# Pooled attention and a GELU layer: scores of 64 pools of both token kinds in one matmul, the other 8 pools in column tiles, k turned by a transposing DMA

## The chip, the core and the metric

The kernel runs on one core of a Trainium2 chip. A core has TensorE (PE, matmuls; a separate record PEld for its weight loads), ScalarE (ACT), VectorE (DVE), GpSimd (POOL) and SyncE (SP). SP, ACT and POOL can issue DMA transfers. The metric is the device time of one execution in microseconds. The kernel before takes 307.78 us (median of three runs, 307.62 to 308.16).

## The reference

Eight batches, eight heads, 576 tokens, head size 64. k and v are averaged over groups of 8 tokens, which gives 72 pools. Then attention of every token over the 72 pools, and a layer with GELU over all 4608 tokens:

```
k_p = k.reshape(B, H, 72, 8, 64).mean(axis=3)       # v_p likewise
scores = 1/sqrt(64) * q @ k_p.T                      # [576, 72] per batch and head
attn = exp(scores - max) / sum
x = (attn @ v_p), heads side by side: [4608, 512]
h = x @ w_in                                         # [4608, 2048]
out = gelu_tanh(h) @ w_out                           # [4608, 512]
```

## The kernel before

**Layout.** `xT` holds the attention's result with the 512 features on partitions (four blocks `ko`, one for each pair of heads) and all tokens along the row. The layer runs over nine groups `g` of 512 tokens. In each group a first product (`p1_mm`, line 332: 16 blocks `fo` of 128 hidden features, four matmuls each, 512 tokens wide), the GELU of each block (`gelu`, line 338, on ScalarE, PSUM to `gT`), and a second product (`p2_mm`, line 343: four blocks of 128 tokens, 16 matmuls each), whose result `store` (line 349) copies to `osb` on VectorE and sends out in four DMAs from SP.

**Attention beside it.** While group `g` is worked on, batch `nb = g + 1` goes through its attention, for g = 0 to 6. Batch 0 has its own code ahead of the loop. In the first product's part, VectorE sums k and v over 8 tokens (`k_steps`, `v_steps`; plan at lines 467 to 473) in three halving additions; TensorE transposes the summed k (`trans_k`, line 196: five transposes), and VectorE copies them into `kTs`. There are two copies of `kT` for a batch, one for each token kind `c` (even and odd tokens): q is transposed in pieces of 128 columns, which are two tokens of 64 features, so even tokens sit on partitions 0 to 63 and odd ones on 64 to 127, and the `kT` of the other half is zero. One transfer, `trans_q_dma` (line 221), transposes q on SP for batches 2 and up.

In the second product's part the matmuls of attention are laid between those of `p2_mm` at written positions `m` (0 to 63; lines 506 to 517; `seq` and `todo`). For each (c, pr), pr being a pair of heads: `qk` (line 234) gives the scores of two heads into PSUM banks 2 and 3, two matmuls 288 tokens wide; `expo` takes exp on ScalarE; `av` (line 254) multiplies by v, whose weights carry 8.0 in 64 further columns, so that one matmul gives both the sum over pools and the denominator, into banks 4 and 5 or 6 and 7 by turns; `norm` (line 265) makes the reciprocal on ScalarE by two logarithms and an exponential; `mult` (line 273) writes `xT` on VectorE in two halves. Heads 4 to 7 have their v sums on partitions 64 to 127, and use 128 rows of pools with zeros between (`pool_rows`).

**Order.** The order on each engine is that of the program text. Tiles carry semaphores, and an engine waits at the instruction that needs one. ScalarE loads a table of functions at each change between GELU and exp (`act_set`). Banks for the products: `h_bank` (line 319) and `o_bank`.

**Loads.** `load_next` (line 449) issues the loads of batch g + 2: q, then its transpose, then a one-element copy on POOL (`gate`) that waits for the transpose, then k, the last 8 pools of v, and the rest of v. All of these loads are issued by POOL. `load_v(1)` (line 422) is issued by SP after a one-column memset during the start-up. `v_moves` (line 148) moves the last 8 pools of v between partitions, in two small DMAs on SP.

The last block of the last group is computed in two column ranges, of 384 and 128 columns; each is stored by four DMAs, two on SP and two on ACT.

The softmax here doesn't subtract the row's maximum and nothing guards it: scores larger than these inputs give would overflow.

## Time and profile before

| what | value |
|---|---|
| median of three runs | 307.78 us |
| profiled execution: its own time | 307.9 us |
| its span in the profile | 306.1 us |
| PE busy | 296.8 us (97%), 1528 matmuls |
| ACT busy | 219.0 us (72%) |
| DVE busy | 150.5 us (49%) |
| POOL busy | 35.0 us (11%) |
| granted TensorE clock | 1.0 of full speed |
| DMA | 41.12 MB, 30806 packets |
| software queue (POOL), SP's queue, ACT's queue | 24.38, 15.14 and 1.31 MB |

The span runs from the first to the last instruction that the profile records; the execution's own time is 1.8 us longer. A matmul's busy time is modelled, and matmuls overlap, so what a stage costs is read from the starts of matmuls in the timeline. A group line gives the line of the code, the engine, the operation, the output and input tiles with their sizes, the count, busy time and mean ns. A timeline line gives start, length, engine, line and operation, and in brackets how long the engine stood idle ahead of it and what released it. The DMA view gives the packets of each queue within a window: q0 is the software queue that POOL feeds, q1 belongs to SP, q10 to ACT.

### The profile page before, as it was taken

How to read it: one execution, taken by the hardware profiler on the slowest of the kernel's cores; microseconds unless marked ns; L12 is line 12 of the kernel's file. 1: busy time of each engine (PE TensorE's matmuls, PEld its weight loads, DVE VectorE, ACT ScalarE, POOL GpSimd, SP SyncE). 2: the span in 40 equal slices, each digit the busy share in tenths (PEclk: the TensorE clock that was granted, in tenths of full speed). 3: DMA queues.
4: the chain of work that ended last, by engine and by line, in shares of the span. 5: the costliest groups of instructions: out<-in, count | busy, mean ns of one | idle time of the engine just before them, and what ended most of it. 6: DMA issues, size and time to landing. Idle time of an engine off the chain costs nothing.

```text
span 306.1 us, 4354 instructions
## 1 busy us (share of the span) xinstructions
PE 296.8 (97%) x1528; PEld 157.6 (51%) x1557; DVE 150.5 (49%) x336; ACT 219.0 (72%) x402; POOL 35.0 (11%) x67
## 2 busy tenths in 40 slices
PE   8999899999999999999999999999999999999994
PEld 3555455555555555555555555555555555445543
DVE  5885757572577057805682559245932630120012
ACT  1687489867987798779977898789868986206500
POOL 7102002305003200320014000400000000000000
PEclk9999999999999999999999999999999999999999
DMA  7999987977955962696159827672101210121022
GB/s 221 266 254 264 227 171 139 310 168 184 257 138 113 278 154 53 118 279 154 35 112 250 181 61 103 203 153 71 35 1 36 59 44 0 36 70 35 2 68 69
DMA packets 30806, 41.12 MB, mean 134 GB/s; under 512 B 18176, under 2 KB 18432, under 8 KB 29888
## 3 DMA queue, kind: packets, MB, share of 16 engines
q0 software_dynamic: 7568, 24.38, 33.7%
q1 hardware_dynamic: 22528, 15.14, 21.1%
q10 hardware_dynamic: 688, 1.31, 1.3%
q8 instruction: 12, 0.20, 0.3%
q14 instruction: 10, 0.08, 0.1%
HBM read 36.70 MB, written 9.44 MB: 151 GB/s over the span
## 4 chain that ended last, share of the span: by engine, by line
PE 87%; DMA 11%; issue 1%; ACT 0%; DVE 0%; POOLq 0%
PE PS L344 40%; PE PS L335 37%; DMA qb<-in_q_dram 11%; PE PS L238 5%; PE PS L260 4%; PE PS L173 1%; PE PS L203 0%; ACT e L246 0%; ACT ld L268 0%; ACT ld L267 0%; DVE osb L353 0%; POOLq L550 0%
## 5 line engine op out<-in xcount | busy, mean ns | idle before, releaser
L344 PE MATMUL PS<-w_out_b,gT 128*128 128x512 bf16 (+2 forms) x577 | 133.9, 373 | 0.7
L335 PE MATMUL PS<-xT,w_in_b 128*128 128x512 bf16 x563 | 126.6, 379 | 0.7
L341 ACT ACTIVATE gT<-PS 128x512 bf16<-128x512 f32 x144 | 81.2, 603 | 48.1 <-PE PS L335 48.0
L335 PEld LDWEIGHTS <-w_in_b 128*128 128x128 bf16 x576 | 64.7, 113 | 57.2
L344 PEld LDWEIGHTS <-gT 128*128 128x128 bf16 x592 | 57.0, 97 | 55.7 <-issue 0.4
L353 DVE COPY osb<-PS 128x512 f32<-128x512 f32 (+2 forms) x37 | 25.1, 677 | 98.2 <-PE PS L344 78.6
L278 DVE TENSOR_TENSOR xT<-PS,rc 64x288 bf16<-64x288 f32 x112 | 50.9, 455 | 31.7 <-ACT rc L270 27.5
L246 ACT ACTIVATE e<-PS 72x576 bf16<-72x576 f32 (+1 forms) x64 | 41.0, 647 | 8.8 <-PE PS L238 7.9
L238 PE MATMUL PS<-qT,kT 128*72 128x288 bf16 (+1 forms) x128 | 25.8, 286 | 0.9 <-ACT qT L213 0.6
L270 ACT ACTIVATE rc<-ld 128x288 f32<-128x288 f32 x56 | 24.8, 444 | 1.8
L313 ACT ACT_TABLE_LOAD x17 | 21.8, 1283 | 4.3 <-issue 4.1
L267 ACT ACTIVATE ld<-PS 64x288 f32<-64x288 f32 x56 | 22.8, 408 | 1.3
L268 ACT ACTIVATE ld<-PS 64x288 f32<-64x288 f32 x56 | 22.5, 402 | 1.4
L260 PE MATMUL PS<-e,vp 72*128 72x288 bf16 (+1 forms) x112 | 23.1, 286 | 0.0
L138 DVE TENSOR_TENSOR kt<-kt 128x1280 f32<-128x1280 f32 (+5 forms) x18 | 18.9, 1048 | 7.6 <-DMA kt<-in_v_dram 4.6
L238 PEld LDWEIGHTS <-kT 128*72 128x72 bf16 (+1 forms) x128 | 13.2, 105 | 15.1 <-DVE qT L215 1.2
L453 POOL COPY gate<-qT 1x2 bf16<-1x2 bf16 x6 | 1.0, 174 | 138.5 <-DMA qT<-qb 138.5
L138 DVE TENSOR_TENSOR vt<-vt 128x1024 f32<-128x1024 f32 (+1 forms) x16 | 15.3, 956 | 1.7 <-DMA vt<-in_v_dram 1.4
L183 DVE COPY kT<-PS 64x288 bf16<-64x288 bf16 (+2 forms) x48 | 13.0, 318 | 6.2 <-PE PS L173 6.0
L260 PEld LDWEIGHTS <-vp 72*128 72x128 bf16 (+1 forms) x112 | 11.0, 98 | 3.8
L365 PE MATMUL PS<-idle 128*128 128x512 bf16 x32 | 10.4, 468 | 1.6 <-DVE idle L126 1.2
L76 POOL DMA_DIRECT2D kt<-in_v_dram x14 | 8.0, 586 | 0.1
(48 smaller groups left out, 88.8 us busy)
## 6 DMA issues: line engine op xcount, KB each, us to landing
out_dram<-osb SPq DMA_DIRECT2D x140, 64.0 KB
kt<-in_k_dram POOLq DMA_DIRECT2D x7, 1024.0 KB, 6.0
vt<-in_v_dram POOLq DMA_DIRECT2D x12, 512.0 KB, 8.7
qb<-in_q_dram POOLq DMA_DIRECT2D x7, 576.0 KB, 11.8
w_in_b<-in_moe_w_in_dram POOLq DMA_DIRECT2D x2, 1024.0 KB, 16.8
w_out_b<-in_moe_w_out_dram POOLq DMA_DIRECT2D x4, 512.0 KB, 19.3
vt<-in_v_dram SPq DMA_DIRECT2D x3, 512.0 KB
kt<-in_k_dram POOLq DMA_DIRECT2D x7, 128.0 KB, 6.0
```

Of the source, the lines that this page charges most:

```text
L138: nc.vector.tensor_tensor(out=o, in0=a, in1=b, op=ALU.add)
L238: nc.tensor.matmul(out=PS[:n, bank + e, :CH].rearrange("j (t p) -> j t p", p=32), lhsT=kTs[b % 2][c][:, h, :n], rhs=qTs[b][:, h // 4, :, h ...
L246: nc.scalar.activation(out=e[:n], in_=PS[:n, bank:bank + 2, :CH], func=ACT.Exp, scale=1.0 / 64.0)
L260: nc.tensor.matmul(out=PS[:, bank + x, :CH], lhsT=window(vps[b % 2][:n], 2 * pr + x), rhs=e[:n, x, :], start=True, stop=True)
L267: nc.scalar.activation(out=ld[0:64], in_=PS[64:128, bank, :CH], func=ACT.Ln)
L268: nc.scalar.activation(out=ld[64:128], in_=PS[0:64, bank + 1, :CH], func=ACT.Ln)
L270: nc.scalar.activation(out=rc, in_=ld, func=ACT.Exp, scale=-1.0)
L278: nc.vector.tensor_tensor(out=xT[rows, pr, col:col + CH], in0=PS[rows, bank + x, :CH], in1=rc[rows], op=ALU.mult)
L335: nc.tensor.matmul(out=PS[:, h_bank(g, fo), c0:c1], lhsT=w_in_b[fo // 8][:, ko, q * 512 + j:(q + 1) * 512:4], rhs=xT[:, ko, r0 + c0:r0 + c ...
L341: nc.scalar.activation(out=gTs[g][:, fo, :], in_=PS[:, h_bank(g, fo), :], func=ACT.Gelu_apprx_tanh)
L344: nc.tensor.matmul(out=PS[:, bank, c0:c1], lhsT=gTs[g][:, fo, r * 128:(r + 1) * 128], rhs=w_out_b[:, fo, c0:c1], start=(fo == 0), stop=(fo ...
L353: nc.vector.tensor_copy(out=osb[:, c0:c1], in_=PS[:, bank, c0:c1])
```

## The change

Batches 0 and 1 keep the old path, with 72 rows of pools for all heads (`pool_rows` is gone, v sums of heads 4 to 7 are written to partitions 0 to 63, and `kTs`, `vps`, `vz` and `ones` shrink to match). For batches 2 to 7 (`KX = 2`):

- k is loaded with its first 64 pools on partitions, four heads on each half, in rows of 2 KB (`load_k_dma`); VectorE writes its sums twice into `kz` (64 partitions), so that each head has a block for even and one for odd tokens with zeros in the other half; one transposing DMA on SP turns all of it into `kx` (`trans_k_dma`). The five TensorE transposes and the copies into `kTs` go.
- `main_scores`: for each head one matmul with 128 columns of weights gives the scores of the first 64 pools for even tokens (rows 0 to 63) and odd tokens (rows 64 to 127). `main_expo` writes its exponentials into rows 0 to 63 of `eT`, for one token kind at a time.
- `rem_scores`: the last 8 pools, eight matmuls (one for each head) of 16 columns of weights, written at partitions 0, 32, 64 and 96 of banks 6 and 7. `rem_expo`: one exponential over all of it, then eight DMAs on SP that move the rows to partitions 64 to 71 of `eT`.
- `av_main` is `av` on `eT`, with pairs of heads in the outer order and token kinds in the inner. Positions `m` are new; the last `av_main` comes after the second product.
- `load_next` for batches 3 and up is issued in the first product's part, after the k sums; its gate waits for `kx`, and q comes last; q's transpose is issued on SP at m = 30.
- In the start-up, `load_v(1)` comes after four more memsets, and v of batch 1 is summed in two halves, the second at m = 18; POOL clears `kz`.
- The last block's two column ranges are stored by one DMA each (the attention writes the last 128 tokens in another order), and `osb` has 5 buffers in place of 6.

The diff, without the parts that only follow from the 72 rows:

```diff
--- before.py
+++ after.py
...
-    opool = ctx.enter_context(tc.tile_pool(name="op", bufs=6))
+    opool = ctx.enter_context(tc.tile_pool(name="op", bufs=5))
...
+    KX = 2
...
     def load_k(b, engs):
...
+        engs[-1].dma_start(out=kts[b % 2][0:64, KR], in_=rows[64:])
...
+    def load_k_dma(b):
+        rows = k[b].rearrange("h (j l) d -> j h (l d)", l=8)
...
-            engs[-1].dma_start(out=kts[b % 2][32 * i:32 * i + 32, KR], in_=rows[64:, 4 * i:4 * i + 4])
+            nc.gpsimd.dma_start(out=kts[b % 2][64 * i:64 * i + 64, 0:KR], in_=rows[0:64, 4 * i:4 * i + 4])
+        nc.gpsimd.dma_start(out=kts[b % 2][64:128, KR], in_=rows[64:])
+        rows = v[b].rearrange("h (j l) d -> j h (l d)", l=8)
+        nc.gpsimd.dma_start(out=kts[b % 2][0:64, KR], in_=rows[64:])
...
+    kz = consts.tile([64, H + 1, 2, 2 * D], BF16, name="kz")
+    eT = consts.tile([Sp, H, 2, CH], BF16, name="eT")
...
+    def k_steps_dma(b):
+        t = kts[b % 2]
+        k0, k1 = (kz[:, :, e, e * D:e * D + D] for e in range(2))
...
+        def third(o, p0, c):
+            p = slice(p0, p0 + 64)
+            return lambda: add(o, t[p, c, 0:64], t[p, c, 64:128])
...
+        return [lambda: add(t[:, :, 0:256], t[:, :, 0:256], t[:, :, 256:512]),
+                lambda: add(t[:, :, 0:128], t[:, :, 0:128], t[:, :, 128:256]),
+                third(k0[:, 0:4], 0, slice(0, KR)), third(k0[:, 4:H], 64, slice(0, KR)),
+                third(k0[:, H], 64, KR), lambda: nc.vector.tensor_copy(out=k1, in_=k0),
+                lambda: trans_k_dma(b), third(kps[b % 2][0:64, KR], 0, KR)]
...
+    kxs = {}
...
+    def trans_k_dma(b):
+        kxs[b] = bp.tile([128, 2 * H + 2, 64], BF16, name="kx", bufs=1)
+        nc.sync.dma_start_transpose(out=kxs[b], in_=kz.rearrange("p h e c -> p (h e c)"))
...
     def v_moves(b):
...
-        for i in range(2):
-            nc.sync.dma_start(out=vps[b % 2][64 - 64 * i:72 - 64 * i, 4 * i:4 * i + 4, 0],
-                              in_=kps[b % 2][32 * i:32 * i + 32, KR])
+        nc.sync.dma_start(out=vps[b % 2][64:Sp, :, 0], in_=kps[b % 2][0:64, KR])
...
+    def v_half(b, i):
...
+        p = slice(64 * i, 64 * i + 64)
+        t = vts[b % 2][p]
+        add(t[:, :, 0:256], t[:, :, 0:256], t[:, :, 256:512])
+        add(t[:, :, 0:128], t[:, :, 0:128], t[:, :, 128:256])
+        add(vps[b % 2][0:64, 4 * i:4 * i + 4, 0], t[:, :, 0:64], t[:, :, 64:128])
...
     def v_steps(b):
...
         def main():
...
-                add(w[p, 4 * i:4 * i + 4], t[p, :, 0:64], t[p, :, 64:128])
+                add(w[0:64, 4 * i:4 * i + 4], t[p, :, 0:64], t[p, :, 64:128])
...
+    def rem_scores(b):
+        kf = kxs[b].rearrange("p b j -> p (b j)")
+        for h in range(H):
+            i, x = h % 4, h // 4
+            nc.tensor.matmul(out=PS[32 * i:32 * i + 16, 6 + x, :CH].rearrange("j (t p) -> j t p", p=32),
+                             lhsT=kf[:, 2 * H * 64 + h::H], rhs=qTs[b][:, x, :, 32 * i:32 * i + 32],
+                             start=True, stop=True)
...
+    def rem_expo(b):
+        r = ep.tile([128, 2, CH], BF16, name="er", bufs=1)
+        nc.scalar.activation(out=r, in_=PS[:, 6:8, :CH], func=ACT.Exp, scale=1.0 / 64.0)
+        for i0 in (0, 2):
+            for c in range(2):
+                for i in (i0, i0 + 1):
+                    nc.sync.dma_start(out=eT[64:Sp, i:H:4, c, :], in_=r[32 * i + 8 * c:32 * i + 8 * c + 8])
...
+    def main_scores(b, pr):
+        kf = kxs[b].rearrange("p b j -> p (b j)")
+        for x in range(2):
+            h = 2 * pr + x
+            nc.tensor.matmul(out=PS[:, 2 + x, :CH].rearrange("j (t p) -> j t p", p=32),
+                             lhsT=kf[:, h * 128:(h + 1) * 128],
+                             rhs=qTs[b][:, h // 4, :, h % 4 * 32:h % 4 * 32 + 32],
+                             start=True, stop=True)
...
+    def main_expo(b, c, pr):
+        nc.scalar.activation(out=eT[0:64, 2 * pr:2 * pr + 2, c, :], in_=PS[64 * c:64 * c + 64, 2:4, :CH],
+                             func=ACT.Exp, scale=1.0 / 64.0)
...
+    def av_main(b, c, pr, bank):
+        for x in range(2):
+            nc.tensor.matmul(out=PS[:, bank + x, :CH], lhsT=window(vps[b % 2], 2 * pr + x),
+                             rhs=eT[:, 2 * pr + x, c, :], start=True, stop=True)
...
     def mult(b, c, pr, bank):
...
+        n = CH if col + CH < N else CH - 128
...
-            nc.vector.tensor_tensor(out=xT[rows, pr, col:col + CH], in0=PS[rows, bank + x, :CH],
-                                    in1=rc[rows], op=ALU.mult)
+            nc.vector.tensor_tensor(out=xT[rows, pr, col:col + n], in0=PS[rows, bank + x, :n],
+                                    in1=rc[rows, :n], op=ALU.mult)
+        if n < CH:
...
+            for x in range(2):
+                rows = slice(x * 64, (x + 1) * 64)
+                nc.vector.tensor_tensor(out=xT[rows, pr, N - 128:].rearrange("k (p t) -> k t p", t=4),
+                                        in0=PS[rows, bank + x, n:CH].rearrange("k (t p) -> k t p", t=4),
+                                        in1=rc[rows, n:].rearrange("k (t p) -> k t p", t=4), op=ALU.mult)
...
-    nc.vector.memset(vts[1][:, 0, 0:1], 0.0)
-    load_v(1, [nc.sync])
...
+    nc.vector.memset(vts[1][:, 0, 0:1], 0.0)
+    load_v(1, [nc.sync])
...
-        nc.vector.memset(w[0:64, H // 2:], 0.0)
-        nc.vector.memset(w[0:8, H // 2:], 8.0)
+    nc.gpsimd.memset(kz, 0.0)
...
         def load_next():
...
-            load_q(g + 2)
-            trans_q_dma(g + 2)
-            nc.gpsimd.tensor_copy(out=gate, in_=qTs[g + 2][0:1, 1, TP - 1, 0:2])
-            load_k(g + 2, [nc.gpsimd])
+            if nb >= KX:
+                nc.gpsimd.tensor_copy(out=gate, in_=kxs[nb][0:1, 2 * H + 1, 0:2])
+            if nb < KX:
+                load_q(g + 2)
+                trans_q_dma(g + 2)
+                nc.gpsimd.tensor_copy(out=gate, in_=qTs[g + 2][0:1, 1, TP - 1, 0:2])
+            if g + 2 >= KX:
+                load_k_dma(g + 2)
+            else:
+                load_k(g + 2, [nc.gpsimd])
...
-        if 0 < g and g + 2 < B:
+            if nb >= KX:
+                load_q(g + 2)
...
+        if 0 < g and nb is not None and nb < KX:
...
-            kk = k_steps(nb)
+            kk = k_steps(nb) if nb < KX else k_steps_dma(nb)
...
-            if g:
+            if nb >= KX:
+                plan = {0: kk + ([load_next] if g + 2 < B else []), 7: vv[:1], 8: vv[1:]}
+            elif g:
...
             else:
...
-                plan = {0: kk, 12: tq[:1], 13: tq[1:2] + tk, 14: tq[2:3], 15: tq[3:] + vv}
+                plan = {0: kk, 12: tq[:1], 13: tq[1:2] + tk, 14: tq[2:3], 15: tq[3:] + [lambda: v_half(1, 0)]}
...
+        if nb is not None and nb >= KX:
+            at(2, rem_scores, nb)
+            at(2, rem_expo, nb)
+            for pr, m in enumerate((6, 17, 31, 44)):
+                at(m, main_scores, nb, pr)
...
+            pairs = [(c, pr) for pr in range(PR) for c in range(2)]
+            for n, m in enumerate((23, 26, 33, 39, 47, 55, 60, 64)):
+                at(m, av_main, nb, *pairs[n], 4 + 2 * (n % 2))
+            for n, m in enumerate((6, 6, 17, 17, 33, 39, 47, 55)):
+                at(m, main_expo, nb, *pairs[n])
+            for n, m in enumerate((23, 26, 33, 39, 47, 55, 60, 64)):
+                at(m, norm, nb, *pairs[n], 4 + 2 * (n % 2))
+            for n, m in enumerate((28, 34, 42, 50, 57, 62, 65, 66)):
+                at(m, mult, nb, *pairs[n], 4 + 2 * (n % 2))
+            if g + 2 < B:
+                at(30, trans_q_dma, g + 2)
+        elif nb is not None:
+            if g == 0:
+                at(18, v_half, 1, 1)
...
     for c0, c1, bank in ((0, 384, o_bank(g, 3)), (384, DM, 4)):
...
-        store(g, 3, bank, c0, c1)
+        osb = opool.tile([128, c1 - c0], F32, name="osb")
+        nc.vector.tensor_copy(out=osb, in_=PS[:, bank, c0:c1])
+        b, col = divmod(N - 128, S)
+        t = col % CH // 32
+        rows = out[b * S:(b + 1) * S].rearrange("(p t e) d -> e p t d", t=TP, e=2)
+        (nc.sync if c0 else nc.scalar).dma_start(out=rows[col // CH, :, t:t + 4, c0:c1],
+                                                 in_=osb)
...
```

## Prediction

> **What bounds the kernel now.** I read the page first, then the windows of one steady stretch, its timeline, and last the DMA view of short windows.
>
> The page, engine totals and the chain that ended last:
>
> ```profile
> PE 296.8 (97%) x1528; PEld 157.6 (51%) x1557; DVE 150.5 (49%) x336; ACT 219.0 (72%) x402; POOL 35.0 (11%) x67
> ...
> PE 87%; DMA 11%; issue 1%; ACT 0%; DVE 0%; POOLq 0%
> ```
>
> TensorE is the chain except for 11% at the start, which is the load of q. One cycle (token group 4) in two windows, its first product (from 151.13) and its second (from 165.23); columns are length, then busy time of each engine:
>
> ```profile
> 151.13:165.23 14.10, 14.05 (x70) 7.50 (x70) 9.85 (x24) 10.74 (x19) 4.40 (x8) 1.00 0.59 154
> 165.23:182.97 17.74, 17.63 (x95) 9.50 (x96) 7.75 (x16) 15.90 (x32) 0.00 (x0) 1.00 0.64 138
> ```
>
> PE has no hole. A run of 512-wide matmuls starts one every 0.216 us (seven in 1.51 in the chain), so 64 take 13.80; the first window adds 0.30 for five transposes of k, the second 3.94 for 32 attention matmuls 288 wide: 0.123 each. Cycle 31.8 us. But ScalarE fills 15.90 of the second window's 17.74, so PE is the bound with ScalarE close behind. The timeline of that window and of the hand-over before it:
>
> ```profile
> 157.36 1.42 SPq L151 DMA_DIRECT2D vp<-kp  x2
> ...
> 166.04 1.28 ACT L313 ACT_TABLE_LOAD   x1
> ...
> 167.34 0.65 ACT L246 ACTIVATE e<-PS 72x576 bf16<-72x576 f32 x1
> ...
> 174.06 0.69 DVE L353 COPY osb<-PS 128x512 f32<-128x512 f32 x1 [0.29 <-PE PS L344]
> ...
> 174.78 0.45 DVE L278 TENSOR_TENSOR xT<-PS,rc 64x288 bf16<-64x288 f32 x1
> ```
>
> An exponential of 576 per row costs 0.65 whether 72 or 128 rows; it cannot start before 2.11 us into the stage (last gelu, table load). SP needs 0.7 per small move. A product copy (0.69) goes ahead of the next pair of multiplications (0.94) on VectorE.
>
> Last, the DMA view of two windows that each begin when SP issues a 256 KB store: one while POOL's loads of k, v, q run, one without loads:
>
> ```profile
> q0 software_dynamic: 238, 0.57, 106.8%
> ```
>
> ```profile
> q1 hardware_dynamic: 124, 0.19, 39.4%
> ```
>
> The first is 106.66 to 109.4: in 2.7 us not one packet of SP's queue moved. In the second (234.02 to 236) 124 of its 192 packets (the whole went from 234.5 to 237) were through after 2 us. The same start at 170.34 waited 2.0 for its first packet, at 74.82 about 2.7, at 202.18 (v rows of 2 KB, loads nearly over) 0.6. The two v moves issued at 32.90 under load had their packets from 36.5 to 40.
>
> **What the Trainium skill says.** "DMA: Bandwidth & Descriptors", section "Issuing engines are not separate DMA queues": transfers issued by SP, ACT and POOL end on the same 16 engines and interleave. The windows above agree, and show that a small one waits 2 to 3 us there. "TensorEngine Tiling (Array Packing)", "Key Properties": tiles run in parallel, but changing the mode drains the array; "TensorE: Matmul & The Clock Gate", "Measured speedup vs the span model", gives 2.38x for three column tiles. No run here shows either under load.
>
> **The change, part by part** (per cycle; six cycles, for batches 2 to 7, change; u is time from the second product's start).
>
> *PE work.* Removed: 16 score matmuls (16 x 0.123 = 1.97) and 5 transposes (0.30). Added: 8 main score matmuls 128 columns wide (0.98) and 8 remainder matmuls of 16 columns. Those cost 0.25 if four tiles fully overlap, 0.98 + two drains (say 1.2) if not; from the skill's 2.38x, 0.98/2.4 = 0.41, I take 0.45 with drains. The 16 value matmuls stay. Net -0.84.
>
> *ScalarE.* Eight exponentials become nine of the same row length, +0.67, with the normalisations unchanged (1.3 each): 9 x 0.67 + 8 x 1.3 = 16.4 from 2.11 on. The schedule, not the total, decides.
>
> *The new wait: eight SP moves.* The remainder exponential runs 2.11 to 2.78; SP issues eight moves from 2.85, 0.69 each (the v moves' row). Ends of issue: second 4.23, fourth 5.61, sixth 6.99, eighth 8.37. The value matmuls of (half 0, heads 0-1) need the second, (half 1, heads 0-1) the fourth, heads 2-3 the sixth and eighth. Without a wait PE would reach them at m=23: 23 x 0.216 + 0.45 + 2 x 0.246 = 5.90; m=26: 6.80; m=33: 8.8; m=39: 10.4.
> Idle queues: landing 1.9 after issue (the transpose of q: issue ends 157.26, POOL's gate passes 159.18). Second 6.13 (PE waits 0.2), fourth 7.51 (0.5), rest in time: 0 to 0.7, taken 0.4.
> But loads now run just then. POOL's gate is tied to k's transpose: k sums start after the last multiplication (about 2.5 into the first product), take 1.49+0.83 and five small ones, about 3.9, the transpose at most 4.7: 9.5 to 11. Loads then move data from about 11.5 for 12.5 us (before: 160.9 to 173.4), that is u = -2.3 to 10.2: k and v in 2 KB rows until u of about 6, then q. I take landing 2.2 after issue behind k and v, 3.3 behind q. Second 6.43: wait 0.53. Then fourth is needed at 7.33, lands 7.81: 0.48. Sixth needed at 9.82, lands 10.29: 0.47. Eighth in time. Sum 1.48. Behind the waiting matmul on PE stands the whole product; behind that ScalarE's normalisation. Bounds: 0 (the moves get through as on an idle queue at its best) to 3.1 (every move waits 3.6 more than its issue, as the v moves at 32.90).
>
> *New bank waits.* Value matmuls alternate between two bank pairs, so number n needs multiplication n-2. Number 5 (m=55) needs multiplication 3, which stands behind the copy of m=47: copy starts 0.19 after m=48, +0.69 +0.94 = 1.82 and a hand-off of 0.05 to 0.1; PE is there after 7 x 0.216 = 1.51: wait 0.38. Number 7 (m=64) follows number 5 by 9 x 0.216 + 0.25 = 2.2; normalisation and multiplication of number 5 take 0.2 + 1.35 + 0.95 = 2.5: wait 0.35. Number 3 likewise 0.14 when no DMA wait has covered it. Bounds 0 (if hand-offs are faster or copies pass earlier) to 1.2.
>
> *Sums.* Loads run in five cycles: -0.84 + 1.48 + 0.73 = +1.37 each, +6.9. The sixth has none: -0.84 + 0.40 + 0.87 = +0.43.
>
> *Start.* v of batch 1 is issued about 3.7 later. It moved 1.05 MB beside q of batch 1, and PE waited for that q:
>
> ```profile
> 33.73 0.45 PE L203 MATMUL PS<-identb,qb 128*128 128x128 bf16 x5 [1.41 <-DMA qb<-in_q_dram]
> ```
>
> With about half of the 3 us less sharing, q lands up to 1.4 earlier: -1.3. What is late next: v of batch 1 (from 33 to about 36.5, needed near 37, so covered; if not, 1 back) and, in the first changed cycle, k of batch 2, landed at 59.96 as before, + 3.9 + up to 4.7 = 68.5, just when PE asks for it (54.3 + 14.2). The memset of the new tile on POOL sits before q of batch 2, which is queued behind other loads: nothing. Fewer VectorE copies in the start-up end in the same wait for q: nothing.
>
> *End.* The last stores are one DMA per queue instead of two on each (0.4 per issue): -0.4. Transposing q on SP at m=30 may hold SP until its q lands (u of about 10 to 12), with 12 stores behind it; they need 12 x 0.43 = 5.2, and five output buffers hold them; k's transpose comes 6.4 into the next cycle: covered; without the cover, 1 to 3 a cycle. VectorE loses 3.4 of kT copies and gains small sums, beside idle time: nothing.
>
> Total: 6.9 + 0.4 - 1.3 - 0.4 = +5.6 on the profiled execution's 307.9 (span 306.1 and 1.8 around it): 313.5. The median is 0.1 below that: 313.4.
>
> **Rivals.**
> (a) The moves slip through the loads, DMA wait 0: -0.84 + 0.87 = 0 a cycle, and start and end leave -1.7: 306.1, or 308 if the start gives nothing. For it: landing is idle-like at 202.18. Against: four other starts under load. It decides if the second move lands within 1.7 of its issue's end and the fourth within 1.2. This is the case on the faster side, and its price is the start's 1.3 and the end's 0.4.
> (b) Moves starve as the v moves did: waits 3.1, -0.84 + 3.1 + 0.73 = +3.0 in five cycles = 15, + 0.4 - 1.7: 321.6. For it: 106.66. Against: those waits stood behind 8 KB and 4.6 KB rows, the new k rows are 2 KB.
> (c) ScalarE is the bound: it needs 1.28 + 16.4 + 1.28 between gelu phases, against the 17.0 of PE and 3.65 to the next gelu; 1.5 of slack, so only with idle time in front. It would show as +0.5 a cycle, 309 to 310 alone.
> (d) Column tiles do not overlap: +0.75 a cycle, but the moves' wait shrinks by as much; alone (with a) 310.
>
> **How the numbers follow.** Waits as priced (310 to 317): 0.50. Starved (317 to 324): 0.25. (a): 0.15 below 307.2 and 0.06 within the bound. (c) or (d) without DMA waits: 0.04, slower. The bound is 0.2%, 0.6 us: what a measurement here can tell. Slower 0.79, within 0.06, faster 0.15. Range from (a)'s middle to most of (b): 306.8 to 321; the likeliest case's own is 310 to 317.
>
> **What would show it.** Right: PE idle ahead of the value matmuls, released by DMA into the new tile, 1 to 3 us in each of five cycles and much less in the sixth; VectorE releases of 0.3 to 0.4 at the sixth and eighth; cycle 33.2; remainder matmuls within 0.5; the wait for q gone near 33. Wrong: cycles of 31.8 or less with DMA releases absent, k's transpose late, or the loads over before u = 3.

## The result, and the profile after

The changed kernel takes 350.12 us (median of four runs, 349.98 to 352.18) against 307.72 for the kernel before on the same chip (307.62 to 308.16): ratio 1.139, 95% interval 1.135 to 1.143. The forecast was 313.4, range 306.8 to 321. The direction was right; the size of one wait was not, and an effect that follows from it was left out.

The page of the changed kernel: engine totals, the TensorE clock by slice, the chain that ended last.

```profile
PE 310.6 (89%) x1527; PEld 154.1 (44%) x1527; DVE 144.7 (42%) x283; ACT 221.7 (64%) x408; POOL 37.5 (11%) x67
...
PEclk9999989996999969998999969996799999999999
...
PE 64%; DMA 22%; ACT 7%; DVE 3%; issue 2%; POOL 1%; SPq 1%; ACTq 0%; DVEq 0%; POOLq 0%
```

TensorE carried 87% of the chain before and carries 64% now. The share of DMA doubled, and the clock, which was 9 in every slice before, falls in six places. The waits of the whole execution, with total, number of times and longest:

```profile
PE PS L322 <- DMA eT<-er: 27.2, 8, 5.5
...
PE PS L286 <- DMA vp<-kp: 2.0, 1, 2.0
```

L322 is the value matmul (`av_main`); `eT<-er` are the eight small moves. One cycle (token group 4) in the two windows that the prediction showed of before, first product and second product:

```profile
175.27:189.61 14.34, 14.34 (x68) 7.33 (x65) 8.86 (x16) 11.55 (x21) 3.40 (x7) 1.00 0.35 69
189.61:214.73 25.12, 20.27 (x95) 9.41 (x95) 7.58 (x16) 15.60 (x32) 1.19 (x2) 0.86 0.75 159
```

These windows meet at the first remainder matmul, 0.52 behind the first matmul of the second product (189.09), from which the prediction counts u. Counted from there, the first product takes 13.8 (14.1 before, with the five transposes), and the second 25.6 in place of 17.7. In the second window PE is busy 20.27 of 25.12, at a mean clock of 0.86 (third number from the end). Its timeline:

```profile
189.61 0.44 PE L295 MATMUL PS<-qT,kx 128*16 128x288 bf16 x8
...
191.20 0.65 ACT L301 ACTIVATE er<-PS 128x576 bf16<-128x576 f32 x1
191.87 6.17 SPq L305 DMA_DIRECT2D eT<-er  x8
...
199.91 0.77 PE L322 MATMUL PS<-eT,vp 72*128 72x288 bf16 x2 [4.72 <-DMA eT<-er]
```

Eight remainder matmuls in 0.44, the exponential and the issue of the moves are where they were forecast. The data are not: the first value matmul starts 8.0 after the first move was issued, and it is the only one of this cycle that waits. The DMA view of 191.9 to 198 names one data queue only (packets, MB, share of the engines):

```profile
q0 software_dynamic: 448, 1.32, 101.8%
```

In 6.1 us POOL's queue moved 448 packets and SP's not one. The first packet of a move starts at 198.2, when k's and v's loads are nearly through. From there on the moves pass beside the load of q, although q had been issued ahead of them (190.06 against 191.87); the same view of 198.5 to 201.5:

```profile
q0 software_dynamic: 249, 0.57, 98.6%
q1 hardware_dynamic: 130, 0.07, 11.6%
```

The other four loaded cycles show the same order, with first packets of the moves at 81.2, 119.8, 159.7 and 238.0. Then the clock; the half-clock stretch of each loaded cycle (length, busy time of PE, clock third from the end), and what follows one of them:

```profile
80.05:86.87 6.82, 3.61 (x11) 1.50 (x11) 0.91 (x2) 2.50 (x6) 0.00 (x0) 0.50 0.88 184
121.00:127.83 6.83, 5.47 (x16) 2.20 (x16) 0.91 (x2) 2.77 (x7) 0.00 (x0) 0.50 0.75 154
161.97:165.38 3.41, 3.24 (x10) 1.28 (x9) 0.91 (x2) 2.45 (x6) 0.00 (x0) 0.50 0.64 150
199.51:206.34 6.83, 6.43 (x19) 2.79 (x19) 1.71 (x4) 3.31 (x8) 0.00 (x0) 0.50 0.65 139
237.06:247.30 10.24, 6.46 (x19) 2.71 (x19) 1.70 (x4) 3.31 (x8) 0.00 (x0) 0.50 0.92 184
...
207.00:214.90 7.90, 7.78 (x42) 3.84 (x41) 4.72 (x11) 7.15 (x17) 0.00 (x0) 1.00 0.43 95
```

In these stretches matmuls 512 wide start 0.43 apart in place of 0.216, so half of PE's busy time is lost: 1.6 to 3.2 us a cycle, 2.5 in the mean. That is the second loss in each cycle.

The table gives, for every kernel, the median and, from the timeline of its profiled execution, where the second group's first product starts and how long the six cycles are from there (start to start; the first five have loads beside them, the sixth has none).

| kernel | median us | second group | five loaded cycles | sixth |
|---|---|---|---|---|
| before | 307.72 | 55.6 | 31.8 31.8 31.8 31.8 31.8 | 31.8 |
| after | 350.12 | 57.9 | 38.8 40.1 38.5 39.5 41.0 | 33.2 |
| e1_early_v | 349.78 | 58.2 | 40.8 38.8 39.9 38.8 39.9 | 33.3 |
| e2_noload | 310.65 | 58.6 | 31.4 32.1 31.6 31.5 31.5 | 33.3 |
| e3_spin | 338.71 | 56.9 | 40.6 36.6 37.2 36.8 37.1 | 33.3 |
| e4_late_vq | 313.54 | 58.5 | 31.4 32.0 32.6 31.8 32.5 | 33.2 |
| e5_all_late | 325.18 | 58.9 | 31.4 36.7 32.1 33.4 33.1 | 36.6 |
| e6_late_tail | 313.55 | 56.5 | 33.8 32.0 32.7 31.5 33.4 | 31.5 |
| e7_late_tail_v | 315.58 | 54.9 | 37.3 32.0 32.9 31.5 32.9 | 31.5 |
| e8_kqv_tail_v | 307.18 | 55.4 | 31.4 31.7 32.3 31.5 31.5 | 32.4 |
| e9_kqv_tail | 310.38 | 56.9 | 31.4 31.7 32.2 31.5 31.6 | 32.2 |
| e10_half_k | 306.23 | 58.2 | 31.4 32.0 31.6 31.5 31.9 | 31.5 |
| e11_act_moves | 354.83 | 57.0 | 41.4 40.5 40.6 39.0 40.3 | 34.4 |

For after, the span grew by 348.1 - 306.1 = 42.0: start +2.3, five loaded cycles +38.6 (7.7 each), sixth +1.4, last stretch -0.3. A loaded cycle's 7.7 is -0.84 of matmuls (as forecast) + 27.2 / 5 = 5.4 of waiting + 2.5 of half clock, and 0.6 that is left, near the 0.5 that e2 leaves for bank waits.

### The profile page after: what moved, and what is told of

It is laid out like the page before. It is cut to its first block, busy times and chain, and to the rows that moved or that the text cites. A ratio compares the mean times of both kernels' runs of the same rounds, so it can differ in the third digit from the quotient of the medians.

```text
span 348.1 us, 4413 instructions
## 1 busy us (share of the span) xinstructions
PE 310.6 (89%) x1527; PEld 154.1 (44%) x1527; DVE 144.7 (42%) x283; ACT 221.7 (64%) x408; POOL 37.5 (11%) x67
## 3 DMA queue, kind: packets, MB, share of 16 engines
q0 software_dynamic: 8512, 24.39, 32.6%
## 4 chain that ended last, share of the span: by engine, by line
PE 64%; DMA 22%; ACT 7%; DVE 3%; issue 2%; POOL 1%; SPq 1%; ACTq 0%; DVEq 0%; POOLq 0%
PE PS L404 32%; PE PS L413 26%; DMA eT<-er 12%; DMA kt<-in_v_dram 6%; PE PS L322 4%; DMA vp<-kp 3%; ACT L381 2%; DVE xT L341 1%; ACT eT L317 1%; PE PS L311 1%; ACT er L301 1%; DVE osb L418 1%; ACT rc L332 1%; ACT ld L330 1%; ACT ld L329 1%
## 5 line engine op out<-in xcount | busy, mean ns | idle before, releaser
L413 PE MATMUL PS<-w_out_b,gT 128*128 128x512 bf16 (+2 forms) x592 | 149.8, 394 | 0.0
L418 DVE COPY osb<-PS 128x512 f32<-128x512 f32 x35 | 24.2, 692 | 128.9 <-PE PS L413 120.5
L341 DVE TENSOR_TENSOR xT<-PS,rc 64x288 bf16<-64x288 f32 (+1 forms) x112 | 49.9, 445 | 52.6 <-ACT rc L332 49.6
L322 PE MATMUL PS<-eT,vp 72*128 72x288 bf16 x96 | 24.9, 321 | 28.9 <-DMA eT<-er 27.2
L317 ACT ACTIVATE eT<-PS 64x576 bf16<-64x576 f32 x48 | 30.8, 642 | 12.5 <-PE PS L311 12.0
L322 PEld LDWEIGHTS <-vp 72*128 72x128 bf16 x96 | 10.2, 106 | 45.3 <-issue 31.5
L150 DVE TENSOR_TENSOR vt<-vt 128x1024 f32<-128x1024 f32 (+3 forms) x18 | 17.1, 952 | 1.1 <-DMA vt<-in_v_dram 0.7
L273 ACT ACTIVATE e<-PS 72x576 bf16<-72x576 f32 x16 | 9.9, 644 | 4.6 <-PE PS L266 4.5
L311 PE MATMUL PS<-qT,kx 128*128 128x288 bf16 x48 | 10.6, 306 | 0.0
L82 POOL DMA_DIRECT2D kt<-in_k_dram x12 | 7.5, 629 | 2.1 <-issue 1.8
```

What stands on the lines that cost most here:

```text
L150: nc.vector.tensor_tensor(out=o, in0=a, in1=b, op=ALU.add)
L317: nc.scalar.activation(out=eT[0:64, 2 * pr:2 * pr + 2, c, :], in_=PS[64 * c:64 * c + 64, 2:4, :CH], func=ACT.Exp, scale=1.0 / 64.0)
L322: nc.tensor.matmul(out=PS[:, bank + x, :CH], lhsT=window(vps[b % 2], 2 * pr + x), rhs=eT[:, 2 * pr + x, c, :], start=True, stop=True)
L341: nc.vector.tensor_tensor(out=xT[rows, pr, col:col + n], in0=PS[rows, bank + x, :n], in1=rc[rows, :n], op=ALU.mult)
L413: nc.tensor.matmul(out=PS[:, bank, c0:c1], lhsT=gTs[g][:, fo, r * 128:(r + 1) * 128], rhs=w_out_b[:, fo, c0:c1], start=(fo == 0), stop=(fo ...
L418: nc.vector.tensor_copy(out=osb, in_=PS[:, bank])
```

## The experiments

The theory after the result: (1) the moves wait behind the loads that POOL has issued ahead of them, some 6 us more than their own time; (2) PE's idle time halves its clock afterwards; (3) the sixth cycle's surplus is the split multiplication of the last batch; (4) the start-up loses its 2.3 to the move of batch 1 that stands behind the load of v of batch 1. The rivals: the moves are slow of themselves; the clock's fall costs nothing of its own; the surplus is the forecast bank waits; the transfers of the start-up only trade places.

### e1_early_v: the load of v of batch 1 at its old place

The change puts this load not only behind the memsets but behind three of batch 0's value matmuls and multiplications as well (issue at 22.75 in place of 19.03). This run undoes that.

```
     mult0(0, 0, 4)
+    nc.vector.memset(vts[1][:, 0, 0:1], 0.0)
+    load_v(1, [nc.sync])
...
-    nc.vector.memset(vts[1][:, 0, 0:1], 0.0)
-    load_v(1, [nc.sync])
     for w in vps:
```

> Against the changed kernel's 350.1. Only the load of v for batch 1 goes back to its old place in the start-up. Theory: in the start-up the move of v's last 8 pools stood behind that load on SP's queue (issued at 30.75, landed near 41.6), so the first cycle ends 2.0 to 2.5 earlier, with a wait of about 1.4 for q back: 347.4 to 348.4. Rival: the start-up lost its time to something else (the clock, v itself): within 0.5 of 350.1.

Measured 349.78 (345.91 to 351.24), ratio to before 1.130 (1.124 to 1.135). The four runs spread over 5.3 us, so they neither show nor exclude a gain of 2. In the profiled execution (351.03) the second group starts at 58.2, not earlier than in the kernel after. The wait for q of batch 1 is back, and longer than before (1.41 there), and a window behind it shows the clock:

```profile
34.65 0.45 PE L235 MATMUL PS<-identb,qb 128*128 128x128 bf16 x5 [2.23 <-DMA qb<-in_q_dram]
```

```profile
34.00:38.00 4.00, 3.30 (x21) 2.09 (x23) 2.11 (x7) 0.60 (x1) 0.00 (x0) 0.75 1.07 215
```

In this execution v is no longer late and q is. The DMA engines are full there (their share, second from the end, is 1.07). As far as these executions show, the old place and the new one only choose which wait is seen; a place in between does better in e7 and e8, below.

### e2_noload: no loads of batches 3 to 7

This kernel leaves out the loads of k, v and q of batches 3 to 7 and computes on the data that lie there; everything else stays, the moves too.

```
-            if g + 2 >= KX:
-                load_k_dma(g + 2)
-            else:
-                load_k(g + 2, [nc.gpsimd])
+            if nb >= KX:
+                qs[g + 2] = qs[2]
+                return
+            load_k_dma(g + 2)
             load_v(g + 2, [nc.gpsimd])
-            if nb >= KX:
-                load_q(g + 2)
```

> Leaves out the loads of k, v and q for batches 3 to 7 (those batches work on what is in the tiles, so the output is not the reference's). Theory: the eight moves wait behind POOL's loads on the DMA engines; without loads the five long cycles (38.5 to 41.0) become like the sixth or a little shorter, 32.5 to 33.2, so 314 to 318. Rival: eight small moves on SP are slow by themselves: no change, 348 to 351.

Measured 310.65, ratio 1.011 (1.008 to 1.013), better than the theory's lower end. The only piece of the chain with a move, out of five cycles (start, length):

```profile
109.53 1.95 DMA eT<-er
```

With nothing ahead of it, what PE waits for is there 1.95 us after the issue, as the prediction took for idle queues, and PE waits 0.5 in all. The chain of the kernel after has five such pieces of 7.92 to 9.05. The moves are not slow of themselves. Four of the five loaded cycles are 31.4 to 31.6: matmuls alone would make it 31.84 - 0.84 = 31.0 by the prediction's prices, so about 0.5 a cycle is left for bank waits, where 0.87 was priced for a cycle without DMA wait. The weight loads of the value matmuls name VectorE's multiplication as their releaser ten times, 4.0 us in all.

### e3_spin: 20 idle matmuls ahead of the first value matmul

```
+        if (c, pr) == (0, 0) and b < B - 1:
+            spin(20, bank)
         for x in range(2):
             nc.tensor.matmul(out=PS[:, bank + x, :CH], lhsT=window(vps[b % 2], 2 * pr + x),
```

> Twenty 512-wide matmuls on zeros (4.3 us) are added ahead of the first value matmul of batches 2 to 6, where PE waits 4.7 for the moves. Theory: the wait also lets the TensorE clock fall to half for some 6 us, which costs 2 to 3 a cycle; with PE busy the clock stays up: 336 to 341. Rival: the clock costs nothing, because ScalarE and VectorE set the pace after the wait: 349 to 352.

Measured 338.71 (338.02 to 339.74), ratio 1.102 (1.100 to 1.105): 11.4 us less than after, with work added. In the profiled executions 9.5 of it are in the loaded cycles and 1.05 in the start-up, where the clock did not fall this time. In a late cycle PE is kept busy while the moves are out, and the clock stays at 1.00 in the windows behind:

```profile
191.04 4.48 PE L431 MATMUL PS<-idle 128*128 128x512 bf16 x20
...
196.27 0.55 PE L324 MATMUL PS<-eT,vp 72*128 72x288 bf16 x2 [0.75 <-DMA eT<-er]
```

```profile
197.00:200.00 3.00, 3.00 (x19) 1.56 (x17) 1.60 (x3) 2.84 (x7) 0.00 (x0) 1.00 0.65 156
```

The later four cycles are 36.6 to 37.2 in place of 38.5 to 41.0. The first did not gain (40.6 against 38.8): there the moves landed later than the spinning lasted, PE waited three times (1.17, 1.02, 0.23), and the clock fell to 0.50 for a stretch all the same. So the half clock is a loss of its own, and it is reached through the idle time.

### e4_late_vq: v and q of the next batch behind the last move

```
             if g + 2 >= KX:
                 load_k_dma(g + 2)
...
+        def load_late():
+            nc.gpsimd.tensor_copy(out=gate2, in_=eT[64:Sp, H - 1, 1, 0:2])
+            load_v(g + 2, [nc.gpsimd])
+            load_q(g + 2)
...
+        if nb is not None and nb > KX:
+            trans_q_dma(nb)
...
-                at(30, trans_q_dma, g + 2)
+                at(3, load_late)
```

> Loads of v and q for the next batch wait on POOL for the last of the eight moves; k is loaded where it was; q is turned at the start of the next group. Theory (backlog): only k is ahead of the moves, 1.25 MB instead of 2.9, and nearly over when they start; the wait for the moves falls from 4.7 to 0 to 1 and the clock stays up: 313 to 320. Rival: any load in flight holds the moves as long as before: 345 to 350. Rival: q comes too late and the next cycle waits: PE idle at the remainder scores instead.

Measured 313.54 (313.22 to 314.36), ratio 1.021 (1.018 to 1.023). All the bytes are loaded, and 36.6 of the 42.4 us are gone. The chain has four pieces with a move:

```profile
106.56 3.44 DMA eT<-er
...
138.57 4.13 DMA eT<-er
...
171.09 3.37 DMA eT<-er
...
202.84 4.01 DMA eT<-er
```

With only k ahead (512 KB twice and two small loads) it takes 3.4 to 4.1 from the issue to the first use; with nothing ahead 1.95; with k and v ahead 7.9 to 9.1. The delay follows the bytes of k and v that are issued ahead of the moves.

### e5_all_late: k too

k's loads go from `load_next` into `load_late`, ahead of v and q.

> All loads of the next batch (k, v, q, in this order) are issued behind the last of the eight moves, so the moves meet an idle DMA system. Backlog theory: the moves land about 2 us after their issue, as with the loads left out; no value matmul waits over 0.5 us for them; loaded cycles of 31.3 to 31.8 us and 309 to 311.5 us in all, if k still lands before the next cycle needs it. If k, issued some 8 us later than in the kernel after, comes too late for the next cycle's first steps, the wait moves to VectorE's first add of k and to the transposing DMA, and the time is 312 to 320. If the moves were slow of themselves (rival): cycles stay near 39, 345 to 352.

Measured 325.18 (323.04 to 328.0), ratio 1.055 (1.052 to 1.059), longer than was expected even for a late k. No value matmul waits for a move any more, and two cycles are at 31.4 and 32.1. But the others and the sixth wait somewhere else:

```profile
PE PS L296 <- DMA kx<-kz: 10.9, 5, 3.5
```

The timeline of the second loaded cycle:

```profile
101.56 2.68 SPq L256 DMA_TRANSPOSE qT<-qb  x1
104.35 1.30 SPq L179 DMA_TRANSPOSE kx<-kz  x1
...
108.32 0.44 PE L296 MATMUL PS<-qT,kx 128*16 128x288 bf16 x8 [3.51 <-DMA kx<-kz]
```

The turn of k (`kx<-kz`) stands behind the turn of q in SP's order, and the latter waits for q, the last of the three loads: VectorE was done with k's sums at 97. It isn't k that is late but the transfer put ahead of it. In this cycle half clock came with the wait: 36.7 is 31.4 + 3.5 + 1.8. In the sixth it did not, although the wait there is nearly as long:

```profile
243.45 0.44 PE L296 MATMUL PS<-qT,kx 128*16 128x288 bf16 x8 [3.38 <-DMA kx<-kz]
```

```profile
243.40:247.00 3.60, 3.55 (x24) 1.73 (x25) 0.00 (x0) 1.94 (x3) 0.00 (x0) 1.00 0.02 5
```

So the length of a wait alone does not decide; the last section comes back to it.

### e6_late_tail and e7_late_tail_v: the last batch's multiplication, and v of batch 1

e6 is e4 with the last batch as before the change:

```
-        n = CH if col + CH < N else CH - 128
+        n = CH
```

and the last stores as four DMAs of 32 rows. e7 is e6 with `load_v(1)` behind `mult0(1, 0, 0)`, about 2 us ahead of its place in the kernel after.

> The run with v and q loaded late (313.5), and the last batch's split multiplication and the stores of the last 128 rows put back as before the change. If the split multiplication (1.57 us in place of 0.94) is what the sixth cycle's surplus of 1.4 us over 31.84 is mostly made of: sixth cycle 31.9 to 32.4, last stretch at most 0.4 longer, 312.3 to 313.1 in all. If the bank waits alone make it: sixth cycle stays at 33.0 to 33.3, 313.5 to 314.

> As the run before, and v of batch 1 is loaded about 2 us earlier, between its place before the change and its place after it. If start-up loses its time to the move behind v of batch 1 and the half clock that follows: first product of the second group 1 to 2.5 us earlier (near 56 to 57), 310 to 312 in all. If q of batch 1 comes as much later as v comes earlier (the transfers of the start-up fill the DMA engines in either order): no gain, 312.3 to 313.5.

The sixth cycle falls from 33.22 to 31.50, by more than expected, while the last stretch grows by 0.1. In the kernel after, the split multiplication (L347) is named at the value matmuls of that cycle:

```profile
280.79 0.30 PE L322 MATMUL PS<-eT,vp 72*128 72x288 bf16 x1 [0.18 <-DVE xT L347]
...
285.44 0.30 PE L322 MATMUL PS<-eT,vp 72*128 72x288 bf16 x1 [0.41 <-DVE xT L347]
285.92 0.30 PE L322 MATMUL PS<-eT,vp 72*128 72x288 bf16 x1 [0.18 <-DVE xT L347]
```

The medians did not follow, and both lie above what was expected: e6 313.55, ratio 1.020 (1.017 to 1.024), and e7 315.58, ratio 1.026 (1.023 to 1.029), though its second group started 3.5 us earlier than e4's. The first loaded cycle took it all back; in e7:

```profile
78.80 0.49 PE L323 MATMUL PS<-eT,vp 72*128 72x288 bf16 x2 [3.97 <-DMA eT<-er]
```

e4, e6 and e7 start their second group at 58.5, 56.5 and 54.9, and their first loaded cycles last 31.4, 33.8 and 37.3; the sums are 89.9, 90.3 and 92.2. k of batch 3 is issued at 69.2 in both e4 and e7, and its 1.3 MB hold up whatever moves are issued before they are nearly through: SP begins to issue the moves at 75.07 in e4 and at 71.52 in e7, and their first packets start at 76.5 and 76.1. A PE that gets there earlier issues the moves earlier and waits for the same event, and in e7 it pays the clock too (half clock from 79.5 to 82.9).

### e8_kqv_tail_v, e9_kqv_tail, e10_half_k: loads in the order of need

e8 is e5 with the loads in the order k, q, v, and with the tail and the early v of e7. e9 is e8 with v of batch 1 at the place of the kernel after. e10 is e8 with the first of k's two large loads left in `load_next`, 10 us into the cycle, and the rest behind the moves:

```
             if g + 2 >= KX:
+                load_k_dma(g + 2, 0)
...
         def load_late():
             nc.gpsimd.tensor_copy(out=gate2, in_=eT[64:Sp, H - 1, 1, 0:2])
-            load_k_dma(g + 2)
+            load_k_dma(g + 2, 1)
             load_q(g + 2)
             load_v(g + 2, [nc.gpsimd])
```

> As the run with all loads behind the moves, but in the order k, q, v, with the last batch's multiplication and stores as before the change and v of batch 1 loaded about 2 us earlier. With all loads behind the moves, k's turn stood in SyncE's queue behind q's turn, which waited for q's load, the last of three. If that order is what cost 36.7 and 33.3 us in place of 31.4: q lands before the next cycle starts, no wait for k's turn over 0.5 us, loaded cycles 31.4 to 32, sixth 31.5, second group's start near 55 to 56, 304.5 to 307 in all, ahead of the kernel before. If k itself is too late whatever the order (rival): waits for k's turn of 2 us and more stay in some cycles, 311 to 322.

> The run before with v of batch 1 at its place after the change. Start-up theory (the move of batch 1 behind v of batch 1, and half clock after it): start of the second group 1 to 3 us later than with v loaded earlier, and now, with no load ahead of the moves in the first loaded cycle either, none of it is made up there: 306 to 309. If the first loaded cycle still takes up the difference (it begins with data that land at the same time either way): within 0.5 us of the run before.

> As the run of 307.2 us (all loads behind the moves in the order k, q, v, stores and last multiplication as before the change, v of batch 1 earlier), but the first of k's two large loads goes out at its place of the kernel after, 10 us into the cycle, some 5 us ahead of the moves. If half of k is through when the moves are issued: moves land about 2 us after issue, k's turn is waited for no more, all loaded cycles and the sixth at 31.4 to 31.6, 304.3 to 306 in all, ahead of the kernel before by 0.5 to 1%. If even that half holds the moves up (rival): waits of 0.5 to 1.5 us ahead of the first value matmul, 306.5 to 311.

e8: 307.18 (306.37 to 310.47), ratio 0.9994 (0.998 to 1.001), equal to before, where a gain was expected. The order of the loads was it: the waits of up to 3.5 for k's turn shrink to 0.9 at most (at most 0.5 was expected). e9: 310.38, ratio 1.010 (1.008 to 1.012), a little above what either theory gave; in its profiled execution, the shortest of its six at 308.92, the second group starts 1.5 later than e8's and the cycles are the same, so here the start-up is not made up for. The earlier place of v pays once no load stands ahead of the moves. e10: 306.23 (305.53 to 309.31), ratio 0.9953 (0.9935 to 0.9972), 0.5% faster than before, and 0.2 beyond the slow end of what was expected. Nobody waits for k's turn now, and for the moves PE waits twice:

```profile
110.99 0.28 PE L325 MATMUL PS<-eT,vp 72*128 72x288 bf16 x1 [0.40 <-DMA eT<-er]
...
206.00 0.28 PE L325 MATMUL PS<-eT,vp 72*128 72x288 bf16 x1 [0.35 <-DMA eT<-er]
```

Its six cycles sum to 190.0 against 191.0 before. What its longest execution lost, it lost in the start-up: the profiled one was the longest of seven, 309.31, and it shows q of batch 1 late by 2.1 and the clock at 0.68 behind, where e8's profile has a wait of 0.8 and no such fall:

```profile
34.60 0.45 PE L238 MATMUL PS<-identb,qb 128*128 128x128 bf16 x5 [2.14 <-DMA qb<-in_q_dram]
```

```profile
34.00:38.00 4.00, 3.40 (x21) 2.20 (x22) 1.69 (x6) 0.60 (x1) 0.00 (x0) 0.68 1.07 221
```

### e11_act_moves: two moves on the other queue

```
-                    nc.sync.dma_start(out=eT[64:Sp, i:H:4, c, :], in_=r[32 * i + 8 * c:32 * i + 8 * c + 8])
+                    eng = nc.scalar if (i0, c) == (0, 0) else nc.sync
+                    eng.dma_start(out=eT[64:Sp, i:H:4, c, :], in_=r[32 * i + 8 * c:32 * i + 8 * c + 8])
```

> The kernel after, with the first two of the eight moves issued on ScalarE's queue, right behind the exponential that writes their data, in place of SyncE's. If loads already issued go first whatever queue the small move is on: the first value matmul still waits about 5 us in each loaded cycle, and the time stays at 348 to 353. If only SyncE's queue is held up (behind its own stores): the first value matmul waits under 1 us and the wait moves to the second, which needs the third and fourth move on SyncE's queue; the time is then 345 to 350.

Measured 354.83, ratio 1.154 (1.146 to 1.161), longer than either expectation. ScalarE issues the two that the first value matmul needs, from 196.15, and that matmul waits nearly as long as it did:

```profile
204.91 0.28 PE L323 MATMUL PS<-eT,vp 72*128 72x288 bf16 x1 [4.18 <-DMA eT<-er]
205.50 0.40 PE L323 MATMUL PS<-eT,vp 72*128 72x288 bf16 x1 [0.31 <-DMA eT<-er]
```

From 196.2 to 202.2 the DMA view again has one data queue only:

```profile
q0 software_dynamic: 446, 1.31, 102.5%
```

It is not SP's queue alone that is held up. Of the added 4.7 us some come from the two issues on ScalarE (1.47 together), which delay the next exponential: the sixth cycle, without loads, is 1.2 longer, and the main score matmuls now wait for ScalarE six times, 7.0 in all.

## Why the prediction was wrong, step by step

**PE work, -0.84 a cycle.** Right. The remainder took 0.44 where 0.45 was priced (0.38 from its start to that of the next matmul), so the column tiles overlap (rival d falls), and without loads four cycles are 31.4 to 31.6.

**The moves' issue.** Right in its place, 2.8 into the stage (2.85 in the prediction), and a little short in its length: 6.17 for eight, against 8 times 0.69 = 5.5.

**The moves' landing: the step that failed.** The prediction took "landing 2.2 after issue behind k and v, 3.3 behind q", hence a wait of 1.48 with an upper bound of 3.1. Measured: 7.9 to 9.1 from the first issue to the first use, and a wait of 5.4 a cycle. The mechanism was named, loads running just then, and the wait sat where it was said to sit, but two terms in it were wrong.

The first: the moves were taken to share the engines with the loads from the start. In the prediction's own evidence, the window 106.66 to 109.4 without one packet of SP's queue, lay the other reading, that nothing passes for as long as the large loads ahead keep the engines. It took these windows to agree with transfers that interleave, and this one shows none that do.

The second: the time of these loads was carried over from before, and k and v were to be through at "u of about 6", 8.3 us after their start. But k now comes in rows of 2 KB in place of 8 KB, and it moves more slowly. The DMA view of 99.5 to 101 before and of 189 to 192 after, both within k:

```profile
q0 software_dynamic: 74, 0.61, 96.3%
```

```profile
q0 software_dynamic: 199, 0.75, 105.0%
```

That is 0.41 and 0.25 MB in a microsecond. With both put right the wait can be worked out from the profile of before: k with v's last pools, and v, are 1.31 and 1.05 MB, and the window 106.66 to 109.4, which has no rows of 8 KB, moved 0.57 MB in 2.74 us, so they take 11.3 us; from the start of the loads at u = -2.3 that leads to u = 9.0. The moves' first packet came at 198.2, which is u = 9.1; that it fits so closely is in part luck, since the loads started 0.9 later than forecast.

The upper bound of 3.1 came from two v moves that had their first packet 3.6 us after their issue. They then passed beside a load that was still running; the view of 37 to 40 before:

```profile
q0 software_dynamic: 177, 0.65, 107.0%
q1 hardware_dynamic: 79, 0.01, 3.9%
```

A delay observed once was used as the most that could be. (Counted from the end of each issue, 3.6 makes the bound 2.4 and not 3.1.) Rival (b), starving, was the right one, with a price that was itself too small, and the reason against it was misread: the wait at 106.66 stood behind no row of 8 KB, all 238 packets are smaller.

**The clock: left out.** Nothing in the sum says what TensorE does after a wait. The Trainium skill has it, "TensorE: Matmul & The Clock Gate", section "What's actually happening": after an idle window of about 3.4 us the clock is halved until a busy window has passed. The runs agree that it is halved, and for 3.41 us or a multiple of it, but a window need not be idle from end to end; about 2 us were enough (last section). After waits of 4.7 to 5.5, half clock cost 1.6 to 3.2 us a cycle. With the forecast waits (0.5 three times) it would by these runs hardly have come in. It turned a mean wait of 5.4 into a loss of 7.9, and e3 took back 9.5 us in the five cycles by keeping PE busy.

**Bank waits, 0.38 and 0.35 (and 0.14).** Somewhat too large: 0.5 a cycle in e2 where 0.87 was said for a cycle without DMA wait. (The second is 2.5 - 2.2 = 0.3 by its own sum.) In the kernel after, 0.6 a cycle is left when the moves' wait and the half clock are taken off, where 0.73 was said.

**The sixth cycle, +0.43.** It was +1.39. The bank waits were priced for the usual multiplication of 0.94; the last batch has the split one, 0.66 + 0.91 = 1.57 for each odd pair of value matmuls, which the prediction did not cost at all. Undone, the cycle is 31.50 (e6).

**Start, -1.3.** It was +2.3. The first half was right: PE does not wait for q of batch 1. The "late next" was misjudged: v of batch 1 was called covered, and the small move of `vp`, issued at 30.75, was not followed. It came 10.87 later:

```profile
30.75 10.87 DMA vp<-kp
```

PE then waited 1.99 at 41.76, and the clock fell to 0.57 in the window 42 to 46. It is again a small transfer behind a large one, but here in one queue: v itself is on SP's queue. Its packets run from 26.7 to 38.3, and those of the move from 38.1 on. In that time v and POOL's loads pass packet for packet, so here the sharing is there; the DMA view of 28 to 38:

```profile
q0 software_dynamic: 459, 1.62, 80.0%
q1 hardware_dynamic: 458, 0.90, 26.3%
```

**End, -0.4.** -0.3.

**Rivals.** (a) needs moves that slip through: the undisturbed cycles of e2, e8 and e10 show what it is worth, 31.4 to 31.6, not 31.84. (c), ScalarE as the bound, is not seen: in e2 the value matmuls wait for it twice, 0.3 in all. (Its slack is 17.0 + 3.65 - 18.96 = 1.7, not 1.5.)

## What to carry to other kernels

A small transfer on the critical path is not priced by its own latency alone. Here it waited for the bytes of the large loads issued just ahead of it, divided by the bandwidth at which their rows move, and changing its queue did not help. So look in the trace for windows in which a queue has work and moves no packet, put large prefetches behind the small transfer with a gate, in the order in which they are needed, and let ahead of it only what is through by then. Where TensorE waits some 2 us or more, ask whether half clock follows. And an instruction moved behind a waiting one on the same queue (k's turn behind q's) waits for that one's data too.

## What the runs showed of the hardware that was not expected

**The queues share, but not always.** The Trainium skill, "DMA: Bandwidth & Descriptors", section "Queues, rings and completion order", says that each engine goes round between the queues that have work, a packet at a time. The start-up agrees (459 packets beside 458), and so do the moves once they have begun to pass beside q. But for 6.1 us from the moves' issue 448 packets of POOL's queue passed and none of SP's; e11 had the same with ScalarE's queue. The measurement decides for this case: the small moves, from SBUF to SBUF, started only when the loads of k and v were nearly through. What in the engines makes it so stays open. That older requests go first does not explain it, since q, issued ahead of the moves as well, did not hold them.

**The clock goes by a fixed beat.** In every trace that has half-clock stretches within the run, they last 3.41 us or two or three times that. In the kernel after they begin at 42.50, 80.05, 121.00, 161.97, 199.51 and 237.06, which are whole multiples of 3.41 apart. So the clock seems to be set anew every 3.41 us, and what counts is how much of one such period PE was idle. The two waits of e5 fit this: of the 3.51 in its second cycle 2.8 lie in the period before the clock fell, and of the 3.38 in its sixth 2.0 lie in one period and 1.4 in the next. The start-ups fit too. In after, e1, e2, e4, e5 and e10, 2.0 to 2.6 of idle time lie in one period, and half clock follows; in e3, e6, e9 and e11 the waits of 2.0 to 2.3 leave at most 1.8 in one, and it does not. So the bound lies near 2 us of 3.41. One case stands out: in e3's first loaded cycle 1.7 was enough. The start of the second group follows: 56.5 to 57.0 in e3, e6, e9 and e11, whose start-up is that of the kernel after but without the fall, and 57.9 to 58.9 with it, in after, e2, e4 and e5. This is read from the traces; no run moved a wait across a beat on purpose.
